# Two gated linear-attention blocks on one core: block B's reciprocals through DRAM, its scalings by row halves

## The chip, the cores and the metric

The kernel runs on one core of a Trainium2 chip. The metric is the device time of the whole program in microseconds; lower is better. The kernel before took 183.14 us, the median of three runs (183.08 to 183.65).

## The reference

Input x is [1, 2048, 640] in bf16. Two blocks A and B have weights of the same shapes, 32 heads of 20 columns each; both read A's x.

```python
def _A_ref(x, wqkv, wo):            # _B_ref is the same with B's weights
    q, k, v = ...                   # x @ wqkv, split in 3 x 32 heads x 20
    phi = lambda t: jnp.where(t > 0, t + 1, jnp.exp(t)) + 1e-6
    pq, pk = phi(q), phi(k)
    kv = jnp.einsum("bhsd,bhse->bhde", pk, v)
    z = jnp.einsum("bhsd->bhd", pk)
    num = jnp.einsum("bhqd,bhde->bhqe", pq, kv)
    den = jnp.einsum("bhqd,bhd->bhq", pq, z)[..., None] + 1e-6
    o = num / den
    return ... @ wo                 # o with its heads side by side
x = A_x
g = _sigmoid((x * gate_w).sum(-1, keepdims=True))
return g * _A_ref(x, A_wqkv, A_wo) + (1 - g) * _B_ref(x, B_wqkv, B_wo)
```

## The kernel before

The 2048 rows and 640 columns are cut in blocks of 128 (16 by 5). All tiles but a few DRAM ones stay on chip. `pk` holds phi(k) by rows; `pqT[0]` and `pqT[1]` hold phi(q) of A and B transposed, as [128, 5, 2048]. The order of the work on each engine is the order in which the program emits it: the scheduler is off (`manual_schedule`), and the framework adds the waits.

**The stages.** A's k and q come first, then the rest of A's q by a Strassen product (`q_strassen`). `g_strassen` computes G = x^T pk, from which KV is made with `wv`; in its midst, `z_rows` and `z_pass` sum pk into z, and `rec_pass` computes the denominators with `by_group` and takes their reciprocals through logarithms, with the gate (`ge`) added. Then the same for B. KV times `wo` gives one 640 x 640 matrix M for each block (`m_a`, `m_b`), six row blocks g each, stored to DRAM (`m_store` to `m_rows`) and loaded back in another row order (`m_load`). At the end, `Pair` computes pqT[0] M_A + pqT[1] M_B for eight pairs of row blocks, again by Strassen products p1 to p7.

**The reciprocals.** `rec_pass` leaves `rT`, [128, 512]: partition 32 j + h has head h's reciprocals of rows 512 j to 512 j + 511. For the scaling they must stand as `R`, [128, 4, 512]: partition 4 h + t has head h's, for t of 0 to 3 and all four j. A and B do this in two ways. For A, `norm_load` stores rT to the DRAM tile `r_rows` four times over (512 KB) and loads R from it with one DMA. For B, `norm_spread` multiplies rT with the 0/1 matrix `spread` in four matmuls (tiles exB) and ScalarE copies the result into R. `scale(b, m, part)` then multiplies the columns m of pqT[b] by R on VectorE, over all 2048 rows or a part of them.

**The order of the work around the change.** In `g_strassen(1, ...)`, B's turn, SyncE issues the load of M_A and then three loads of B's `wo` (`load_wo`) just ahead of `rec_pass`. VectorE computes `p_diff` (differences of pqT[0]'s two row halves into D3, a quarter `part[n]` of the first half at a time), scales A's last columns, adds partial products into the second half matrix `GT[1]` (L527 and L587), and scales B's columns: m of 0 and 1 by row halves, 2 and 3 in full, 4 later. `rest` is `kv_low`: the first three KV blocks with their masks, and `tm_first` (the difference of M_A's column halves into TM[0]) for three of five blocks. After `g_strassen`, `m_b` makes M_B's row blocks: two matmuls, then two copies of half a row each, on ScalarE or VectorE. The three upper KV blocks (tile ox, L624, `kv_mm`) stand between `m_b(2)` and `m_b(3)`. They read GT[1], whose last piece is L587's second addition. Then follow `tm_first` for the other blocks, the scaling of m = 4, `p_sums` (sums of pqT[0] and pqT[1] by quarters, k of 1, 2 and 4), the pairs' p1 and p5, the last `p_diff`, and `m_sum` (TM[2], TM[1], TM[3] from the loaded M_B). The pairs' p2, p7 and p6 read M_B, TM[2] and TM[1] in this order.

All the plain loads and stores named here go through SyncE's one queue.

Of the kernel before, what the change touches and what calls it, by code (L numbers as in the profile page):

```python
# [21 lines left out]
HB = 512  # L22
HF = D // 2
TW = 4
NG = 6
K6 = 120
EPS = 1e-6
# [6 lines left out]
def kernel(  # L34
# [52 lines left out]
    def ps(name, slot=None):  # L87

        return banks(ps_raw(name, slot))
# [11 lines left out]
    zE = persist.tile([P, 2 * D], BF16, name="zE")  # L101
    E4 = zE[:, D:2 * D]
    maskE = persist.tile([P, HF], BF16, name="maskE")
    spread = persist.tile([P, P], BF16, name="spread")
    R = persist.tile([P, 4, HB], BF16, name="R")
    kv6 = [persist.tile([P, D], BF16, name="kvA6")[:], zE[:]]
    lift = persist.tile([P, 1], FP32, name="lift")
# [26 lines left out]
    scratch = ctx.enter_context(tc.tile_pool(name="scratch", bufs=1, space=bass.MemoryType.DRAM))  # L134
    m_rows = scratch.tile([D, D], BF16, name="m_rows")
    g_rows = scratch.tile([2 * ST, P], FP32, name="g_rows")
    r_rows = scratch.tile([4, P, HB], BF16, name="r_rows")

    wq_dram = [A_wqkv.rearrange("(c p) f -> p c f", p=P), B_wqkv.rearrange("(c p) f -> p c f", p=P)]
    wo_dram = [A_wo, B_wo]  # L140
# [37 lines left out]
    for r in range(4):  # L178
        rows = slice(32 * r, 32 * r + 32)
        nc.gpsimd.tensor_copy(out=I4[rows], in_=ident[rows, rows])  # L180
    nc.gpsimd.tensor_copy(
        out=spread[:].rearrange("p (h t) -> p h t", t=TW), in_=I4[:, :, None].to_broadcast([P, H, TW])
    )
    nc.gpsimd.memset(maskE[:], 1.0)
    for lo in range(0, HF, K6):
        part = maskE[:, lo:min(lo + K6, HF)]
# [63 lines left out]
    class Phi:  # L250
# [10 lines left out]
                    self.lift(lifted_to, part)  # L261

        def lift(self, to, part):
            nc.scalar.activation(out=to, in_=part, func=ACT.Identity, bias=lift[:])

        def clamp(self):
            nc.vector.tensor_scalar(self.e, self.e, 1.0, EPS, op0=ALU.min, op1=ALU.add)  # L267
# [247 lines left out]
    def g_strassen(b, main, second, spare, rest=None):  # L515

        x11, x12 = [xn[:, k:k + hc, 0:ic] for k in (0, hc)]
        x22 = xn[:, hc:ST, ic:2 * ic]
        b11 = pk[:, 0:hc, 0:HF]
        b21, b22 = [pk[:, hc:ST, n * HF:(n + 1) * HF] for n in range(2)]  # L520
        lo, hi = GT

        def temp(name):
            return work.tile([P, 2, HF], FP32, tag="osb", name=name, bufs=3)

        def add(dst, pt, sb):
            nc.vector.tensor_tensor(out=dst, in0=pt[:, :, 0:HF], in1=sb[:], op=ALU.add)  # L527

        even, odd = ps("gs0", main), ps("gs1", second)
        sel = []  # L530
        g_prod(even, x11, b11, True)
        nc.scalar.copy(out=odd[:, :, 0:HF], in_=even[:, :, 0:HF])
        if b == 0:
            rest()
            zr = z_rows(0, spare)
            sq_sum(1, 0)
            g_prod(even, x12, b21, False)
            nc.scalar.copy(out=lo[:, 0:2, :], in_=even[:, :, 0:HF])
            sq_sum(2, 0)
            x_sum(3)  # L540
        else:
            m_a(5, 2)
            nc.sync.dma_start(out=M[0][:], in_=m_rows[:].rearrange("(p m) d -> p m d", m=DT))
            load_wo(1, nc.sync)
            scale(0, 3)
            zr = z_rows(1, spare)
        g_prod(odd, SX[2], TK[b][2], False, lambda: sel.append(z_pass(b, zr)))
        u2 = temp("u2")
        nc.scalar.copy(out=u2[:], in_=odd[:, :, 0:HF])
        if b == 1:  # L550
            scale(0, 4)
            p_diff(part[0])
            rts = rec_pass(b, sel[0], 2)
            k_sum(1, 1)
            for rows in part[1:3]:
                p_diff(rows)
            g_prod(even, x12, b21, False)
            nc.scalar.copy(out=lo[:, 0:2, :], in_=even[:, :, 0:HF])
            norm_spread(b, rts, (2, spare))
        else:  # L560
            k_sum(0, 1)
            norm_load(rec_pass(b, sel[0], 2))
            x_sum(4)
            for k in (3, 4):
                sq_sum(k, 0)
            tq_sums(1, (0, 1))
        g_prod(odd, SX[3], TK[b][3], False)
        u3 = temp("u3")
        nc.scalar.copy(out=u3[:], in_=odd[:, :, 0:HF])
        if b == 1:  # L570
            for rows, ms in ((slice(0, SH), (0, 1)), (slice(SH, S), (0, 1))):
                for m in ms:
                    scale(b, m, rows)
        even = ps("gs0", main)
        g_prod(even, SX[1], TK[b][1], True)
        add(hi[:, 2:4, :], even, u3)
        if b == 0:
            tq_sums(1, (2, 3))
        else:
            scale(b, 2)  # L580
            scale(b, 3)
        g_prod(odd, x22, TK[b][4], False)
        nc.scalar.copy(out=lo[:, 2:4, :], in_=odd[:, :, 0:HF])
        for ns in ((0, 1),) if b == 0 else ((0,), (1,)):
            g_prod(even, SX[4], b22, False, None, ns)
            for n in ns:
                nc.vector.tensor_tensor(out=hi[:, n, :], in0=even[:, n, 0:HF], in1=u2[:, n], op=ALU.add)  # L587
            if b == 1 and ns == (0,):
                rest()

    def z_rows(b, slot=None):

# [36 lines left out]
    def kv_mask(b, banks, g0, g1):  # L629

        n, hf = rows_in(g0), g0 // 3
        at = slice(blocks[g0].start, blocks[g1 - 1].stop)
        part = slice(at.start - hf * HF, at.stop - hf * HF)
        nc.vector.tensor_tensor(out=kv6[b][:n, at], in0=banks[hf][:n, part], in1=maskE[:n, part], op=ALU.mult)
# [24 lines left out]
    def m_b(g, banks):  # L659

        to = m_block(1, g, banks, held["mb"][:, g, :] if g < DT else None)
        n = to.shape[0]
        for hf, copy in enumerate((nc.scalar.copy, nc.scalar.copy if g in (1, 2, 5) else nc.vector.tensor_copy)):
            copy(out=to[:, hf * HF:(hf + 1) * HF], in_=banks[hf][:n, 0:HF])
        m_store(g, to)

# [10 lines left out]
    def rec_pass(b, zsel, slot):  # L677

        pt = ps(f"den{'AB'[b]}", slot)
        by_group(pt[:, 0, :], zsel, pqT[b])  # L680
        rT = work.tile([P, HB], BF16, tag="rT", name="rT", bufs=1)
        ds = [(slice(n * RB, (n + 1) * RB), work.tile([P, RB], FP32, tag="d1", name="d1")) for n in range(2)]
        for part, d1 in ds:
            nc.scalar.activation(out=d1[:], in_=pt[:, 0, part], func=ACT.Ln, scale=LOGS, bias=tiny[:])
        for part, d1 in ds:
            nc.vector.scalar_tensor_tensor(
                out=d1[:], in0=d1[:], scalar=-2.0 * math.log(LOGS), in1=ge[:, b, part], op0=ALU.add, op1=ALU.add
            )
            nc.scalar.activation(out=rT[:, part], in_=d1[:], func=ACT.Exp, scale=-1.0)
        return rT  # L690
# [4 lines left out]
    def p_diff(rows):  # L695

        up = slice(SH + rows.start, SH + rows.stop)
        add_rows(D3[:, :, rows], pqT[0][:, :, rows], pqT[0][:, :, up], ALU.subtract)
# [12 lines left out]
    def tm_first(cs):  # L711
        add_rows(TM[0][:, cs], M[0][:, cs, HF:D], M[0][:, cs, 0:HF], ALU.subtract)
# [9 lines left out]
        else:  # L722
            add_rows(TM[3][:], b[:, :, lo], TM[1][:], ALU.subtract)

    def norm_load(rT):

        nc.sync.dma_start(
            out=r_rows[:].rearrange("j (h t) n -> (j h) t n", t=TW), in_=rT[:, None, :].to_broadcast([P, TW, HB])
        )
        nc.sync.dma_start(out=R[:], in_=r_rows[:].rearrange("j p n -> p j n"))  # L730

    def norm_spread(b, rT, slots):

        pts = [ps(f"ex{'AB'[b]}", s) for s in slots]
        for j in range(4):
            rows = slice(32 * j, 32 * j + 32)
            nc.tensor.matmul(
                pts[j // 2][:, j % 2, :], lhsT=spread[rows, :], rhs=rT[rows, :], start=True, stop=True,
            )
        for jj in range(2):  # L740
            nc.scalar.copy(out=R[:, 2 * jj:2 * jj + 2, :], in_=pts[jj][:])

    def scale(b, m, part=slice(0, S)):

        rec = R[:].rearrange("p j n -> p (j n)")
        nc.vector.tensor_tensor(out=pqT[b][:, m, part], in0=pqT[b][:, m, part], in1=rec[:, part], op=ALU.mult)
# [195 lines left out]
    with tc.manual_schedule():  # L942
# [113 lines left out]
        def kv_low():  # L1056
            kv = cells(ps("kvB", 2))
            kv_mm(1, kv, range(3))
            kv_mask(1, kv, 0, 2)
            kv_mask(1, kv, 2, 3)  # L1060
            tm_first(slice(0, 3))

        g_strassen(1, 1, 0, 3, kv_low)
        new_stage(None)
# [11 lines left out]
            kv_mm(1, [None, acc["x"][g > 3]], [g], (2, 3, 4, 0, 1))  # L1076
        for g in range(3, 6):
            kv_mask(1, [None, acc["x"][g > 3]], g, g + 1)
        pairs[4].p1(acc["w"][0], (0, 1))
        m_b(3, [acc["w"][1], acc["x"][0]])  # L1080
        pairs[4].p1(acc["w"][0], (2,))
# [3 lines left out]
        pairs[4].p1_out()  # L1085
        m_load(0, 3, nc.sync)
        m_load(3, 6, nc.sync)
        tm_first(slice(3, DT))
        scale(1, 4)
        for rows, ks in ((0, (1,)), (1, (1,)), (2, (1,)), (0, (2, 4))):  # L1090
            p_sums(part[rows], ks)
        for k, to in ((5, None), (6, acc["x"][0]), (7, acc["w"][1]), (2, acc["z"][0]), (3, acc["z"][1])):
            pairs[k].p1(to)
        held["p5"] = wpool.tile([P, 4, HF], FP32, tag="wv", name="p5s")
        pairs[0].p1()
        pairs[2].p5(spare[0])
        pairs[3].p5(acc["w"][1])
        pairs[1].p1()
        pairs[4].p5(spare[0])
        pairs[5].p5(acc["z"][1])  # L1100
        for p in pairs[0:2]:
# [3 lines left out]
        acc["y"] = [bank(inner, f"oy{n}") for n in range(2)]  # L1105
        TM[3] = wpool.tile([P, DT, HF], BF16, tag="wk", name="TM3")
        p_sums(part[1], (2, 4))
        p_diff(part[3])
        for k in (2, 1, 3):
            m_sum(k)  # L1110
        for p in pairs[0:2]:
# [60 lines left out]
```

## Time and profile before

| | before |
|---|---|
| median of three runs | 183.14 us (183.08, 183.14, 183.65) |
| profiled execution: span, first to last instruction | 181.6 us; its own time is not listed apart from that |
| TensorE busy | 177.7 us, 98% |
| VectorE busy | 148.3 us, 82% |
| ScalarE busy | 107.9 us, 59% |
| GpSimd busy | 5.0 us, 3% |
| DMA | 18.85 MB, 104 GB/s on the mean |
| granted TensorE clock | 1.000 |

The profile is of one execution, in microseconds from the first instruction. PE is TensorE, PEld its weight loads, DVE VectorE, ACT ScalarE, POOL GpSimd and SP SyncE. A row of the timeline is: start, length, engine, line of the kernel, operation, out<-in with the tiles' names, shapes, count, and in brackets the idle time before it with what ended it. Several like instructions in a row are one row; then the length runs from the first's start to the last's end. A row of the chain of waits is: start, length, what. A row of DMA issues on the page is: out<-in, queue, count, KB each, and the median us from the issue to the landing. A row of the table by windows is: the window, PE busy, then busy time and count of PE, PEld, DVE, ACT, POOL, then the granted clock, the busy share of the DMA engines and GB/s. Tiles that share memory can show under an older name: SQ is also D3, xT is also the sums' place, and T is a sum of pk.

### The profile page before, as it was taken

The numbers are of one execution on the slowest core, as the hardware profiler recorded it, in microseconds if no ns is written. First come the engines' busy times: TensorE is split into PE (matmuls) and PEld (weight loads), VectorE is DVE, ScalarE is ACT, GpSimd is POOL, SyncE is SP. The second block draws the span as 40 slices with busy tenths as digits, with TensorE's granted clock in tenths as the row PEclk, the third lists the DMA queues.
The fourth block names the chain that finished last, engine by engine and source line by source line (L and its number), as shares of the span: only waits on it lengthen the run. The fifth ranks groups of instructions, "written<-read, shape, count | busy, mean of one in ns | idle before, by whom it ended". The sixth has DMA issues, their size and how long they took to land.

```text
span 181.6 us, 3380 instructions
## 1 busy us (share of the span) xinstructions
PE 177.7 (98%) x1284; PEld 118.5 (65%) x1284; DVE 148.3 (82%) x268; ACT 107.9 (59%) x209; POOL 5.0 (3%) x21
## 2 busy tenths in 40 slices
PE   8999999999999999999999999999999999999993
PEld 3666656655666677676666655765678777777772
DVE  0478988999999896799898987997988988686764
ACT  2066579976884512785868696964814755466210
POOL 8300000000000000000000000000000000000000
PEclk9999999999999999999999999999999999999999
DMA  5995448985102733005000000043901660322132
GB/s 172 298 178 88 93 112 251 370 173 141 48 0 58 244 120 115 0 0 180 5 0 0 0 4 0 13 146 84 291 12 31 176 159 0 110 88 96 72 131 90
DMA packets 21602, 18.85 MB, mean 104 GB/s; under 512 B 9298, under 2 KB 21074, under 8 KB 21586
## 3 DMA queue, kind: packets, MB, share of 16 engines
q1 hardware_dynamic: 20722, 17.82, 35.7%
q10 hardware_dynamic: 864, 0.82, 1.3%
q8 instruction: 10, 0.16, 0.4%
q14 instruction: 6, 0.05, 0.1%
HBM read 11.86 MB, written 4.80 MB: 92 GB/s over the span
## 4 chain that ended last, share of the span: by engine, by line
PE 93%; DMA 4%; DVE 1%; issue 0%
PE gs L510 17%; PE kB L290 12%; PE q L408 11%; PE kA L290 11%; PE qA L343 7%; PE oy L757 6%; PE oz L757 5%; PE ox L757 4%; PE ow L757 4%; PE q L343 3%; DMA wkA<-in_A_wqkv_dram 2%; PE gB L480 2%; PE gA L480 2%; DMA xn<-in_A_x_dram 2%; PE qB L343 1%; PE mA L640 1%
## 5 line engine op out<-in xcount | busy, mean ns | idle before, releaser
L290 PEld LDWEIGHTS <-xT 128*128 128x128 bf16 x320 | 30.9, 97 | 15.4 <-issue 0.4
L267 DVE TENSOR_SCALAR e<-e 128x640 bf16<-128x640 bf16 (+2 forms) x58 | 19.6, 339 | 6.1 <-ACT e L259 5.5
L290 PE MATMUL kB<-wkB,xT 128*128 128x320 bf16 x160 | 24.2, 299 | 0.0
L290 PE MATMUL kA<-wkA,xT 128*128 128x320 bf16 (+1 forms) x160 | 23.4, 299 | 0.2 <-DMA wkA<-in_A_wqkv_dram 0.2
L259 ACT ACTIVATE e<-q 128x512 bf16<-128x512 f32 x26 | 15.7, 603 | 5.2 <-PE q L408 4.1
L510 PEld LDWEIGHTS <-xn 128*128 128x128 bf16 x128 | 12.2, 98 | 6.0 <-issue 1.3
L259 ACT ACTIVATE e<-kA 128x640 bf16<-128x640 f32 x16 | 11.3, 713 | 7.8 <-PE kA L290 7.7
L259 ACT ACTIVATE e<-kB 128x640 bf16<-128x640 f32 x16 | 11.4, 710 | 7.5 <-PE kB L290 7.3
L343 PE MATMUL qA<-xT,wqA 128*128 128x512 bf16 x60 | 13.4, 379 | 0.0
L343 PEld LDWEIGHTS <-wqA 128*128 128x128 bf16 x64 | 7.5, 117 | 5.9
L278 DVE SCALAR_TENSOR_TENSOR pk<-kB,e 128x640 bf16<-128x640 f32 x12 | 9.9, 823 | 1.0
L820 ACT COPY u<-ox 128x320 f32<-128x320 f32 x8 | 3.4, 425 | 11.4 <-PE ox L757 11.4
L757 PEld LDWEIGHTS <-xT 128*128 128x128 bf16 x85 | 8.1, 98 | 2.9
L757 PEld LDWEIGHTS <-pqTA 128*128 128x128 bf16 x85 | 8.0, 98 | 2.8
L762 DVE TENSOR_TENSOR osb<-oz,u 128x320 bf16<-128x320 f32 (+2 forms) x18 | 8.0, 453 | 2.2 <-PE oz L757 1.8
L757 PEld LDWEIGHTS <-pqTB 128*128 128x128 bf16 x80 | 7.8, 98 | 3.0
L510 PE MATMUL gs<-pk,xn 128*128 128x320 bf16 x64 | 9.4, 299 | 0.0
L278 DVE SCALAR_TENSOR_TENSOR pk<-kA,e 128x640 bf16<-128x640 f32 x10 | 8.2, 823 | 0.9
L426 DVE TENSOR_TENSOR q<-q,p 128x512 f32<-128x512 f32 x12 | 8.3, 692 | 0.8 <-PE q L408 0.6
L259 ACT ACTIVATE e<-qA 128x1024 bf16<-128x1024 f32 x6 | 6.2, 1027 | 4.2 <-PE qA L343 3.9
L480 PEld LDWEIGHTS <-xn 128*128 128x128 bf16 x64 | 6.3, 98 | 3.0
L510 PEld LDWEIGHTS <-S 128*128 128x128 bf16 x64 | 6.0, 98 | 2.5 <-issue 0.3
(183 smaller groups left out, 348.1 us busy)
## 6 DMA issues: line engine op xcount, KB each, us to landing
out_dram<-osb SPq DMA_DIRECT2D x14, 160.0 KB, 1.8
xn<-in_A_x_dram SPq DMA_DIRECT2D x3, 640.0 KB, 6.7
wvA<-in_A_wqkv_dram SPq DMA_DIRECT2D x1, 800.0 KB, 12.0
wkB<-in_B_wqkv_dram SPq DMA_DIRECT2D x1, 800.0 KB, 4.5
wqB<-in_B_wqkv_dram SPq DMA_DIRECT2D x1, 800.0 KB, 5.3
wvB<-in_B_wqkv_dram SPq DMA_DIRECT2D x1, 800.0 KB
MA<-m_rows SPq DMA_DIRECT2D x1, 800.0 KB, 5.3
MB<-m_rows SPq DMA_DIRECT2D x2, 400.0 KB, 4.3
```

What stands on the lines that cost most here:

```text
L259: nc.scalar.activation(out=to, in_=part, func=ACT.Exp)
L267: nc.vector.tensor_scalar(self.e, self.e, 1.0, EPS, op0=ALU.min, op1=ALU.add)
L278: nc.vector.scalar_tensor_tensor(out=dst, in0=src, scalar=1.0 + EPS, in1=e, op0=ALU.add, op1=ALU.max)
L290: nc.tensor.matmul(pt[:, hf, 0:n], lhsT=xT[:, c, i * P:(i + 1) * P], rhs=wk[b][:, c, hf * HF:hf * HF + n], start=(c == 0), stop=(c == DT - 1),
L343: nc.tensor.matmul(dst, lhsT=mixed(wq[b][:, c, :], m), rhs=xT[:, c, n * HB:(n + 1) * HB], start=first, stop=last,)
L408: nc.tensor.matmul(dst, lhsT=left(c), rhs=right(c), start=first and k == 0, stop=k == len(cs) - 1, skip_group_check=not first,)
L426: nc.vector.tensor_tensor(out=dst, in0=src, in1=sb, op=ALU.add)
L480: nc.tensor.matmul(pt[:, hf, 0:HF], lhsT=xn[:, i, c * P:(c + 1) * P], rhs=pk[:, i, hf * HF:(hf + 1) * HF], start=(i == 0), stop=(i == ST - 1),
L510: nc.tensor.matmul(pt[:, n, 0:HF], lhsT=left[:, i, n * P:(n + 1) * P], rhs=right[:, i, :], start=(first and i == 0), stop=(i == hc - 1), s ...
L757: nc.tensor.matmul(dst, lhsT=left[:, c, r0:r0 + P], rhs=right[:, c, :], start=(first and c == 0), stop=(c == DT - 1), skip_group_check=not ...
L762: nc.vector.tensor_tensor(out=dst, in0=acc, in1=sb, op=ALU.add)
L820: nc.scalar.copy(out=self.u2[:], in_=self.at("x"))
```

## The change

- B's reciprocals go through DRAM as A's do. `norm_spread`, the matrix `spread` and ScalarE's two copies are gone. The new `norm_store` stores rT once (128 KB), each block to its own DRAM tile; the new `norm_load` loads R with four DMAs of 128 KB, one for each j, whose source repeats each row four times. A uses the same two functions.
- B's scalings are all by row halves (10 instead of 4 halves and 3 full ones) and later: m of 0 and 1, first half, where m of 2 and 3 were; m = 2, first half, in the middle of the last two additions to GT[1]; m of 3 and 4, first half, and 0, second half, behind the KV masks; the other second halves behind `m_load`.
- `tm_first` moves ahead, in one piece, to where the scalings of m of 0 and 1 were, and so does the last `p_diff`.
- `m_b` copies both halves on ScalarE for all g but 0, where g of 3 and 4 had one half on VectorE.
- The first `p_sums` come in the order of quarters 1, 2, 0 instead of 0, 1, 2; p1 of pairs 0 and 1 come together ahead of the first p5, and p5 of pair 3 goes to another PSUM bank.
- The bias of the lifts (`Phi.lift`, L264) is a number instead of a tile.

```diff
-    spread = persist.tile([P, P], BF16, name="spread")
-    r_rows = scratch.tile([4, P, HB], BF16, name="r_rows")
+    r_rows = [scratch.tile([4, H, HB], BF16, name=f"r_rows{b}") for b in "AB"]
...
-            nc.scalar.activation(out=to, in_=part, func=ACT.Identity, bias=lift[:])
+            nc.scalar.activation(out=to, in_=part, func=ACT.Identity, bias=1.0 + EPS)
...
         if b == 1:
             scale(0, 4)
             p_diff(part[0])
-            rts = rec_pass(b, sel[0], 2)
+            norm_store(1, rec_pass(b, sel[0], 2))
+            norm_load(1, range(4))
             k_sum(1, 1)
             for rows in part[1:3]:
                 p_diff(rows)
             g_prod(even, x12, b21, False)
             nc.scalar.copy(out=lo[:, 0:2, :], in_=even[:, :, 0:HF])
-            norm_spread(b, rts, (2, spare))
         else:
             k_sum(0, 1)
-            norm_load(rec_pass(b, sel[0], 2))
+            norm_store(0, rec_pass(b, sel[0], 2))
+            norm_load(0, range(4))
...
         if b == 1:
-            for rows, ms in ((slice(0, SH), (0, 1)), (slice(SH, S), (0, 1))):
-                for m in ms:
-                    scale(b, m, rows)
+            tm_first(slice(0, DT))
+            p_diff(part[3])
...
-            scale(b, 2)
-            scale(b, 3)
+            for m in (0, 1):
+                scale(b, m, slice(0, SH))
...
             if b == 1 and ns == (0,):
                 rest()
+                scale(b, 2, slice(0, SH))
...
-        for hf, copy in enumerate((nc.scalar.copy, nc.scalar.copy if g in (1, 2, 5) else nc.vector.tensor_copy)):
+        for hf, copy in enumerate((nc.scalar.copy, nc.scalar.copy if g else nc.vector.tensor_copy)):
...
-    def norm_load(rT):
-        nc.sync.dma_start(
-            out=r_rows[:].rearrange("j (h t) n -> (j h) t n", t=TW), in_=rT[:, None, :].to_broadcast([P, TW, HB])
-        )
-        nc.sync.dma_start(out=R[:], in_=r_rows[:].rearrange("j p n -> p j n"))
+    def norm_store(b, rT):
+        nc.sync.dma_start(out=r_rows[b][:].rearrange("j h n -> (j h) n"), in_=rT[:])
+    def norm_load(b, js):
+        for j in js:
+            nc.sync.dma_start(
+                out=R[:, j, :], in_=r_rows[b][j][:, None, :].to_broadcast([H, TW, HB])
+            )
...
             kv_mask(1, kv, 2, 3)
-            tm_first(slice(0, 3))
...
             kv_mask(1, [None, acc["x"][g > 3]], g, g + 1)
+        for m, rows in ((3, slice(0, SH)), (4, slice(0, SH)), (0, slice(SH, S))):
+            scale(1, m, rows)
...
-        tm_first(slice(3, DT))
-        scale(1, 4)
-        for rows, ks in ((0, (1,)), (1, (1,)), (2, (1,)), (0, (2, 4))):
+        for m in range(1, DT):
+            scale(1, m, slice(SH, S))
+        for rows, ks in ((1, (1,)), (2, (1,)), (0, (1,)), (0, (2, 4))):
...
-        pairs[0].p1()
+        for p in pairs[0:2]:
+            p.p1()
         pairs[2].p5(spare[0])
-        pairs[3].p5(acc["w"][1])
-        pairs[1].p1()
+        pairs[3].p5(acc["z"][0])
...
         p_sums(part[1], (2, 4))
-        p_diff(part[3])
```

More of the change, by code (lines that the diff above doesn't have):

```diff
@@ L180 @@
         nc.gpsimd.tensor_copy(out=I4[rows], in_=ident[rows, rows])
-    nc.gpsimd.tensor_copy(
-        out=spread[:].rearrange("p (h t) -> p h t", t=TW), in_=I4[:, :, None].to_broadcast([P, H, TW])
-    )
     nc.gpsimd.memset(maskE[:], 1.0)
@@ L723, in m_sum @@
             add_rows(TM[3][:], b[:, :, lo], TM[1][:], ALU.subtract)
-    def norm_load(rT):
-        nc.sync.dma_start(
-            out=r_rows[:].rearrange("j (h t) n -> (j h) t n", t=TW), in_=rT[:, None, :].to_broadcast([P, TW, HB])
[L729 to L738, printed above, removed]
-            )
-        for jj in range(2):
-            nc.scalar.copy(out=R[:, 2 * jj:2 * jj + 2, :], in_=pts[jj][:])
+    def norm_store(b, rT):
[4 more added lines that the diff above has]
+                out=R[:, j, :], in_=r_rows[b][j][:, None, :].to_broadcast([H, TW, HB])
+            )
     def scale(b, m, part=slice(0, S)):
```

## Prediction, made before the result was known

> **What bounds the kernel now.** I read three views in this order: the page's first, second and fourth part, to see which engine sets the end; the chain of waits in order of time around the change, to see whether that engine ever stops; and the timeline of the other engines there, to see how much room each has.
>
> ```profile
> span 181.6 us, 3380 instructions
> PE 177.7 (98%) x1284; PEld 118.5 (65%) x1284; DVE 148.3 (82%) x268; ACT 107.9 (59%) x209; POOL 5.0 (3%) x21
> PE 93%; DMA 4%; DVE 1%; issue 0%
> ```
>
> TensorE is busy for 98% and carries 93% of the chain; the rest of the chain is the first loads and the last additions. VectorE has 82%, so it has room on average, but an average says nothing about one place. The chain around the change (start, length, what):
>
> ```profile
> 128.49 0.33 PE exB L737 x4
> 128.82 7.71 PE gs L510 x56
> ...
> 138.91 0.27 PE mB L640 x2
> 139.18 0.74 PE ox L624 x15
> ```
>
> Each piece begins where the one before ended (128.49 and 0.33 is 128.82, 138.91 and 0.27 is 139.18), in the rows left out too. TensorE does not stop here, so this stretch gets shorter only by matmuls taken out, and longer by every input that comes late. Now VectorE, ScalarE and SyncE beside it (start, length, instruction, in brackets the idle time before it):
>
> ```profile
> 127.23 0.78 ACT L689 ACTIVATE rT<-d 128x256 bf16<-128x256 f32 x2
> 127.56 0.42 SPq L873 DMA_DIRECT2D woB<-in_B_wo_dram  x1
> 128.88 1.56 DVE L693 TENSOR_TENSOR SQ<-pqTA 128x1280 bf16<-128x1280 bf16 x2
> 130.35 2.49 DVE L746 TENSOR_TENSOR pqTB<-pqTB,R 128x1024 bf16<-128x1024 bf16 x4
> 133.38 0.82 DVE L527 TENSOR_TENSOR GT<-gs,u 128x640 bf16<-128x640 f32 x1 [0.54 <-PE gs L510]
> 134.12 2.35 DVE L746 TENSOR_TENSOR pqTB<-pqTB,R 128x2048 bf16<-128x2048 bf16 x2
> 136.57 0.49 DVE L587 TENSOR_TENSOR GT<-gs,u 128x320 bf16<-128x320 f32 x1
> 137.30 0.55 DVE L634 TENSOR_TENSOR zE<-kvB,maskE 120x240 bf16<-120x240 f32 x2 [0.24 <-PE kvB L624]
> 137.78 0.65 DVE L693 TENSOR_TENSOR TM<-MA 128x960 bf16<-128x960 bf16 x1
> 138.40 0.49 DVE L587 TENSOR_TENSOR GT<-gs,u 128x320 bf16<-128x320 f32 x1
> 139.02 0.90 PE L624 MATMUL ox<-GT,wvB 128*120 128x120 bf16 x15
> ```
>
> The place to watch is the last two rows. The second half of GT is added on VectorE until 138.40 + 0.49 = 138.89; the matmuls that read it (ox, the upper KV blocks) start at 139.02, at once. There is no slack between them. Whatever makes that addition later makes TensorE stop.
>
> **The change, part by part.**
>
> *Removed from TensorE:* the four exB matmuls that spread rT over partitions, 0.33 us in the chain. Everything behind them moves up by 0.33 us if its inputs do. The POOL copy that makes the spread matrix was off the chain from the start.
>
> *Removed from ScalarE:* the two copies of exB into R. ScalarE was not late here. The biases of the lifts become a number; whatever ScalarE gains by that is hidden, since the chain gives ScalarE no share at all. Two half-row copies of M_B (g of 3 and 4) move from VectorE to ScalarE.
>
> ```profile
> 141.23 0.74 ACT L664 CAST m<-mB 80x320 bf16<-80x320 f32 x2
> 142.68 0.34 SPq L649 DMA_DIRECT2D m_rows<-m  x1
> ```
>
> ScalarE has eleven copies instead of nine. In a row they take 0.74 / 2 = 0.37 us each, so the last ends at 141.97 + 2 x 0.37 - 0.33 = 142.4 where it was 141.97; its store leaves at 142.68 today. I count zero; without that cover it is 0.4 us on the load of M_B.
>
> *A's half:* the store shrinks from 512 to 128 KB, and the load becomes four loads of 128 KB. The first user is the scaling at 71.44.
>
> ```profile
> 66.89 0.38 SPq L730 DMA_DIRECT2D R<-r_rows  x1
> 71.44 1.22 DVE L746 TENSOR_TENSOR pqTA<-pqTA,R 128x2048 bf16<-128x2048 bf16 x1
> 55.80 2.83 SPq L238 DMA_DIRECT2D ge<-g_rows  x4
> r_rows<-rT SPq DMA_DIRECT2D x1, 512.0 KB, 3.3
> R<-r_rows SPq DMA_DIRECT2D x1, 512.0 KB, 3.8
> m_rows<-MA SPq DMA_DIRECT2D x4, 150.0 KB, 2.0
> ge<-g_rows SPq DMA_DIRECT2D x4, 128.0 KB, 2.9
> ```
>
> Today's load leaves at 66.89, when the store of 3.3 us has landed, so the store left at 63.6. A store of 128 KB is nearest to the 150 KB ones: 2.0 us, landing at 65.6. Four issues took 2.83 us for ge, so the last leaves by 68.0 and lands by 68.0 + 2.9 = 70.9, before 71.44. Zero.
>
> *B's half, the costly part.* Today R is filled on chip and VectorE starts scaling at 130.35. Now R takes a round trip through DRAM. The store cannot leave before rT, 127.23 + 0.78 = 128.01, and SyncE is free of woB at 127.56 + 0.42 = 127.98; so it leaves at 128.0. But it stands behind woB and the load of M_A in the same queue:
>
> ```profile
> 131.00:132.00 1.00, 1.00 (x9) 0.72 (x8) 1.00 (x3) 0.74 (x2) 0.00 (x0) 1.00 0.87 164
> 132.00:133.00 1.00, 1.00 (x10) 0.71 (x8) 0.84 (x2) 0.00 (x0) 0.00 (x0) 1.00 0.11 22
> woB<-in_B_wo_dram SPq DMA_DIRECT2D x2, 300.0 KB, 5.5
> wvA<-in_A_wqkv_dram SPq DMA_DIRECT2D x1, 800.0 KB, 12.0
> woA<-in_A_wo_dram SPq DMA_DIRECT2D x1, 200.0 KB, 10.7
> 28.14 0.98 SPq L863 DMA_DIRECT2D wvA<-in_A_wqkv_dram  x1
> 31.78 0.80 SPq L873 DMA_DIRECT2D woA<-in_A_wo_dram  x1
> ```
>
> The last two columns of the first rows are the busy share of the DMA engines and GB/s: they work until a little after 132. And the queue is served in order: wvA left at 28.14 and landed at 40.1; the small woA part left at 31.78 and landed at 42.5, not ahead of it. So the store lands with woB's end: bounds are 130.0 (128.0 + 2.0, no queue) and 134.6 (132.6 + 2.0, all of its latency after the queue). I take 133.4: woB's second part left before 127.56 and took 5.5 us, so up to 133.0, and the window from 132 to 133 has little of it, so 132.6; the store's 128 KB behind it take 0.8 us at the 164 GB/s of that time. Then the loads: the first leaves at 133.4, the second, which completes the first row half, 0.4 us later, landing 2.0 (the 150 KB rows) to 2.9 us (ge) after: I take 2.5, between them, since a lone load of 512 KB took 3.8. That is 133.4 + 0.4 + 2.5 = 136.3, and with a tenth for the semaphore R's first half is usable at T = 136.4.
>
> What VectorE does meanwhile: tm_first (0.65 + 0.48 in two pieces today) and the last p_diff (0.78, half of the 1.56) fill 130.35 to about 132.1; then the 0.82 addition at 133.05 (up by 0.33). From 133.9 its next instruction is the scaling of row half 0, and VectorE waits for T with the first GT addition, the masks, a third scaling and the second GT addition queued behind. From T on: two half scalings at 2.49 / 4 = 0.62, 1.24; the GT addition 0.45; the masks 0.48 (137.30 to 137.78); one half scaling in the place of tm_first, 0.62 (137.78 to 138.40); the second addition 0.49. It ends at T + 3.28 = 139.7 instead of 138.89. TensorE's ox follows it without slack, so TensorE is **0.8 us later than today**, the 0.33 us it had won included. Break-even is at T + 3.28 = 138.89, T = 135.6; up to T = 135.3 the addition waits for TensorE alone and the whole 0.33 us is kept.
>
> *The later scalings:* seven row halves come after the masks, where today are one full scaling, the two M_B copies and 0.48 of tm_first.
>
> ```profile
> 149.79 0.99 DVE L693 TENSOR_TENSOR TM<-MB,MA 128x1600 bf16<-128x1600 bf16 x1 [0.60 <-DMA MB<-m_rows]
> 150.70 2.07 DVE L693 TENSOR_TENSOR TM<-MB,TM 128x1600 bf16<-128x1600 bf16 x2
> 152.12 0.84 PE L757 MATMUL ox<-TM,xT 128*128 128x320 bf16 x5
> 139.96 0.43 DVE L634 TENSOR_TENSOR zE<-ox,maskE 120x120 bf16<-120x120 f32 x2 [0.18 <-PE ox L624]
> 142.97 2.29 DVE L693 TENSOR_TENSOR pqTA<-pqTA,pqTB 128x1280 bf16<-128x1280 bf16 x3
> ```
>
> Today the p_sums begin at 142.97, and VectorE waits 0.60 us for M_B before 149.79. With the masks ended at 139.96 + 0.43 = 140.4 and 7 x 0.62, they begin at 144.7, 1.8 us later; a p_diff (0.78) is gone from before the m_sums, and the wait (0.60) swallows another part: the m_sums come 1.8 - 0.78 - 0.60 = 0.4 us later. TM1 was done at 150.70 + 2.07 / 2 = 151.7, against 152.12 of its reader: 0.4 us of slack. If TensorE itself is 0.8 us later, VectorE's chain moves with it and M_B's does too (its first copy stands behind the second GT addition): no second bill. If R is in time, TensorE comes 0.33 us earlier than today, and up to 0.4 us may be due here.
>
> *Sum:* 181.6 + 0.8 = 182.4 for the profiled execution. The median of the three runs is 183.14, 1.5 us outside the span; so 183.14 + 0.76 = **183.9 us**.
>
> **The rivals.** *(1) R is in time (T up to 135.3): 183.14 - 0.33 = 182.8 us, not slower.* For it: by the lower bounds, a store that does not queue and a load of 2.0 us, T is 130.0 + 0.4 + 2.0 + 0.1 = 132.5. Against it: the in-order rows above. It decides at T = 135.6. The Trainium skill, "DMA: Bandwidth & Descriptors", Latency and other measured facts, gives 0.6 us to the first byte of a DMA from this queue; an estimate from that page, with 0.3 us for 128 KB, would have the second load land at 134.7 and this rival win. The trace's own loads of 128 KB took 2.9 us, which speaks against it. Chance 0.32.
> *(2) R is later still:* the scalings wait for all four loads, 0.8 us more, or each transfer meets its upper bound, T = 137.2 to 137.9: 184.7 to 185.4 us. Against the first: today the first half scaling started at 130.35, before the second half of R was copied. Chance 0.14.
> *(3) VectorE's late chain binds* though R is in time: the 0.4 us of the late scalings, or the 0.4 us of M_B's copies, meets a TensorE that has no slack left after moving up 0.33 us: 182.8 + 0.4 = 183.2 us. Chance 0.05.
>
> **How the numbers follow.** Forecast (T between 135.9 and 137.0, 183.4 to 184.5): 0.45; rival 1 0.32, rival 2 0.14, rival 3 0.05, and 0.04 for what I don't see. A measurement here tells about 0.3%, 0.55 us. Faster by that would need more than the 0.33 us of matmuls taken out, and no other matmul goes: only the unseen 0.04. Within it lie rivals 1 and 3 and the forecast below T = 136.2 (0.08): 0.45. Slower: the rest of the forecast, 0.37, and rival 2: 0.51. The likeliest is 183.9; the range runs from 182.6, rival 1 with some room for the spread of the runs, to the middle of rival 2, 185.0; the forecast's own is 183.4 to 184.5.
>
> **What would show it.** Right: a VectorE row at the first half scaling of pqTB with idle time before it put down to DMA R<-r_rows, of about 2.5 us, ending near 136.4; then a gap of TensorE before m_b or ox at 138 to 140, of 1.1 us, that the chain of waits gives to VectorE or DMA; no exB rows. Wrong in size: R's loads that land before 135.3 and a chain that is all TensorE. Wrong in place: TensorE stopping first at the readers of TM1 or of M_B near 150, or A's first scaling waiting near 71.

## The result, and the profile after

The changed kernel takes 185.01 us, the median of six runs (184.23 to 187.56), beside 183.11 us of the kernel before on the same chip (183.01 to 183.65). The ratio is 1.009, with an interval of 1.0063 to 1.0117; it leaves out the longest run, in which the clock was lower, as the ratios below leave out every run over 1.5% above the fastest of its kernel. So the change costs 1.2 to 2.1 us. The prediction was 183.9, in 182.6 to 185.0; the median lies at the upper end of that.

From the page of the changed kernel: the span, the busy time of each engine, the slices of TensorE and of its granted clock, the shares of the chain of waits, and the group of B's scalings (busy time and mean ns of one, then the idle time just before and what ended it).

```profile
span 184.7 us, 3382 instructions
PE 179.0 (97%) x1280; PEld 119.3 (65%) x1280; DVE 147.4 (80%) x268; ACT 104.4 (57%) x209; POOL 4.8 (3%) x20
PE   8999999999999999999999999999959999999993
PEclk9999999999999999999999999999996999999999
PE 89%; DMA 6%; DVE 1%; SPq 1%; issue 0%; DVEq 0%
L736 DVE TENSOR_TENSOR pqTB<-pqTB,R 128x1024 bf16<-128x1024 bf16 x10 | 6.3, 682 | 3.3 <-DMA R<-r_rowsB 3.3
```

Four matmuls fewer (1280 for 1284), yet the span is 3.1 us longer. Two slices tell why: in slice 30 TensorE falls to a half, and in slice 31 it is busy again, but its clock is not full. TensorE's share of the chain fell from 93% to 89%; DMA and the issue queues have taken most of it. One thing waits for DMA in the middle of the kernel, the scalings of B, and only once: 3.3 us in one piece. The view of TensorE's waits has the other end (who <- for whom: us, times, longest):

```profile
PE gs L506 <- DVE GT L583: 2.0, 1, 2.0
PE warm L202 <- PEq L1146: 0.8, 1, 0.8
```

TensorE stops once after its warm-up, for 2.0 us, at the last product of `g_strassen` (tile gs), for the first GT addition. The timeline shows what lies between (start, length, instruction, in brackets the idle time before it):

```profile
127.40 0.42 SPq L863 DMA_DIRECT2D woB<-in_B_wo_dram  x1
127.86 0.44 SPq L724 DMA_DIRECT2D r_rowsB<-rT  x1
132.69 0.82 DVE L523 TENSOR_TENSOR GT<-gs,u 128x640 bf16<-128x640 f32 x1 [0.88 <-PE gs L506]
133.72 2.47 SPq L729 DMA_DIRECT2D R<-r_rowsB  x4
136.81 1.29 DVE L736 TENSOR_TENSOR pqTB<-pqTB,R 128x1024 bf16<-128x1024 bf16 x2 [3.29 <-DMA R<-r_rowsB]
138.02 0.49 DVE L583 TENSOR_TENSOR GT<-gs,u 128x320 bf16<-128x320 f32 x1
138.56 2.27 PE L506 MATMUL gs<-pk,MB 128*128 128x320 bf16 x8 [1.98 <-DVE GT L583]
140.86 0.49 DVE L583 TENSOR_TENSOR GT<-gs,u 128x320 bf16<-128x320 f32 x1 [1.30 <-PE gs L506]
```

The store leaves at 127.86 right behind wo, its landing lets the loads go at 133.72, and VectorE stands before the first scaling until 136.81. Behind two scalings comes the first GT addition, and only when it is done does TensorE begin the second half of the product, which writes the tile that this addition reads. (By the code the addition reads the half n = 0 of the tile and these matmuls write the half n = 1; whether a tile for each half would spare the wait was not tried.) The eight matmuls then take 2.27 us, where the first half took 1.25. The table by windows (last three columns: granted clock, busy share of the DMA engines, GB/s) says why:

```profile
138.00:139.00 1.00, 0.44 (x2) 0.24 (x2) 1.00 (x5) 0.00 (x0) 0.00 (x0) 0.81 0.00 0
139.00:140.00 1.00, 1.00 (x5) 0.58 (x4) 0.56 (x1) 0.00 (x0) 0.00 (x0) 0.50 0.00 0
140.00:141.00 1.00, 1.00 (x6) 0.70 (x4) 0.14 (x1) 0.00 (x0) 0.00 (x0) 0.50 0.00 0
141.00:142.00 1.00, 1.00 (x6) 0.74 (x5) 0.85 (x2) 0.76 (x3) 0.00 (x0) 0.50 0.00 0
142.00:143.00 1.00, 1.00 (x18) 0.97 (x17) 0.28 (x1) 1.00 (x4) 0.00 (x0) 0.98 0.21 51
```

Behind the gap the clock is halved: 0.19 + 3 x 0.50 + 0.02 = 1.71 us lost, that is 3.4 us at half clock. To compare programs without their first loads and last stores, I take the time from the start of the first qA matmuls to the start of the last additions and call it the body; the chain of waits has both, of before and of after:

```profile
11.65 4.32 PE qA L343 x20
...
178.15 0.98 DVE osb L762 x3
```

```profile
11.51 4.32 PE qA L339 x20
...
181.26 0.98 DVE osb L752 x3
```

That is 166.50 us before and 169.75 after, 3.25 us more. The terms: -0.33 for exB, +1.98 for the gap, +1.71 for the clock make 3.36. Not every run pays for the clock: of the six, the profiled one (186.43) and the longest have a mean granted clock of 0.991 and 0.990, the other four 0.998 to 1.0 and 184.23 to 185.04 us. A mean of 0.991 over 184.7 us is 1.7 us, one such halved stretch.

### The profile page after: what moved, and what is told of

The parts are those of the page before. It is cut to its first block, busy times and chain, and to the rows that moved or that the text cites. A ratio compares the mean times of both kernels' runs of the same rounds, so it can differ in the third digit from the quotient of the medians.

```text
span 184.7 us, 3382 instructions
## 1 busy us (share of the span) xinstructions
PE 179.0 (97%) x1280; PEld 119.3 (65%) x1280; DVE 147.4 (80%) x268; ACT 104.4 (57%) x209; POOL 4.8 (3%) x20
## 4 chain that ended last, share of the span: by engine, by line
PE 89%; DMA 6%; DVE 1%; SPq 1%; issue 0%; DVEq 0%
PE gs L506 12%; PE kA L286 12%; PE kB L286 12%; PE q L404 11%; PE qA L339 7%; PE oy L747 6%; PE oz L747 6%; PE ox L747 4%; PE ow L747 4%; DMA r_rowsB<-rT 3%; PE q L339 3%; PE gB L476 2%; PE gA L476 2%; DMA xn<-in_A_x_dram 2%; DMA R<-r_rowsB 1%; PE qB L339 1%
## 5 line engine op out<-in xcount | busy, mean ns | idle before, releaser
L736 DVE TENSOR_TENSOR pqTB<-pqTB,R 128x1024 bf16<-128x1024 bf16 x10 | 6.3, 682 | 3.3 <-DMA R<-r_rowsB 3.3
```

## The experiments

Each kernel is timed against the kernel before on the same chip. Line numbers differ by a few between kernels.

**wo behind the round trip.** The changed kernel, but wo's three loads are issued behind the loads of R.

```diff
             nc.sync.dma_start(out=M[0][:], in_=...)
-            load_wo(1, nc.sync)
             scale(0, 3)
...
             norm_load(1, range(4))
+            load_wo(1, nc.sync)
             k_sum(1, 1)
```

> The changed kernel with one edit: the three loads of B's wo are issued behind B's store and loads of R instead of ahead of them. Theory Q (R is late because the store stands behind wo in SyncE's queue): the store leaves near 127.9 as before but lands near 130.2 instead of 133.7, R's first half near 133 instead of 136.8; VectorE's first half scaling starts at 133.6, right behind the 0.82 us addition, TensorE has no gap, and the time is 0.33 us under the kernel before: 182.8 us. Theory L (the late order of the scalings and M_B's copies on ScalarE cost the time): the time stays at 184.3 or more. If wo itself comes late (it is wanted at 137.9), m_b's first matmul waits, and the time lies between, with the gap at m_b.

182.94 us (182.57 to 184.10), before 183.44: ratio 0.9978, interval 0.9959 to 0.9997. Its timeline:

```profile
128.34 0.34 SPq L724 DMA_DIRECT2D r_rowsB<-rT  x1
130.11 1.18 SPq L729 DMA_DIRECT2D R<-r_rowsB  x2
133.99 1.28 DVE L736 TENSOR_TENSOR pqTB<-pqTB,R 128x1024 bf16<-128x1024 bf16 x2
136.44 0.49 DVE L583 TENSOR_TENSOR GT<-gs,u 128x320 bf16<-128x320 f32 x1 [1.16 <-PE gs L506]
```

The same store now takes 1.7 us (128.34 to before 130.11), not 5.8. The first scaling has no bracket: it waits for nothing. The first GT addition waits for TensorE, not the other way round, and TensorE has no gap there. So the whole loss hangs on what stands in front of the store. A repeat on another chip gave 183.04 us (182.38 to 183.85) beside 183.51, ratio 0.9986, 0.997 to 1.0002. By the two ratios that is 0.4 and 0.3 us below before, near the 0.33 us of exB. Of all kernels here this is the fastest; 2 us below the changed one, and below the one before by so little that one of the two intervals still touches 1.

> The kernel with wo behind once more, beside the one with A's old path: 182.6 to 183.2 us, and 0.3 to 0.5 us below the kernel before on this chip (the exB matmuls taken out are 0.33 us).

**The spread on chip again.** The changed kernel with `norm_spread` for B put back; the later scalings, the moved `tm_first` and `p_diff`, ScalarE's copies and A's half stay.

```diff
-            norm_store(1, rec_pass(b, sel[0], 2))
-            norm_load(1, range(4))
+            rts = rec_pass(b, sel[0], 2)
...
+            norm_spread(b, rts, (2, spare))
```

> The changed kernel with B's reciprocals spread on chip again (four matmuls, two copies on ScalarE), all else of the change kept. Theory Q: R is there by 131, no wait on VectorE, no gap on TensorE, the 0.33 us of matmuls are back: 183.1 us, as the kernel before, within 0.3 us. Theory L: the late scalings, tm_first and p_diff ahead, and ScalarE's copies carry the loss: 184.3 us or more, with TensorE waiting for TM1 or M_B near 150.

183.59 us (183.08 to 183.88) beside 183.44, ratio 1.0009, 0.9994 to 1.0023, and in its trace TensorE does not stop between its start and its end. All of the reordering costs nothing that can be told from none. The loss is B's trip through DRAM.

**The DRAM path alone.** The kernel before with `norm_store` and `norm_load` for both blocks, and none of the later scalings.

```diff
-            rts = rec_pass(b, sel[0], 2)
+            norm_store(1, rec_pass(b, sel[0], 2))
+            norm_load(1, range(4))
...
-            norm_spread(b, rts, (2, spare))
```

> The kernel before with the round trip through DRAM alone (A's and B's R by one store and four loads); B's scalings stay where they were, at 130.4. Theory Q: R's first half is usable at 136.8, its last quarter near 138.3; VectorE waits from 130.4 for it, four half scalings, 2.5 us, then the addition to GT that frees the PSUM tile of the next product, which TensorE wants at 135.0, ends near 141: a gap of TensorE of about 5 us, and with the clock at half for 3.4 us behind it another 1.7: 188 to 190 us. Theory L: without the late order the DRAM path costs little: 182.8 to 184 us.

190.37 us (190.09 to 190.63), ratio 1.0377, 1.0347 to 1.0406, a little more than the 188 to 190 that I expected. From its timeline, and then from its windows:

```profile
137.04 2.52 DVE L751 TENSOR_TENSOR pqTB<-pqTB,R 128x1024 bf16<-128x1024 bf16 x4 [6.76 <-DMA R<-r_rowsB]
140.35 2.29 PE L510 MATMUL gs<-pk,MB 128*128 128x320 bf16 x8 [5.49 <-DVE GT L527]
```

```profile
138.00:139.00 1.00, 0.00 (x0) 0.00 (x0) 1.00 (x3) 0.00 (x0) 0.00 (x0) 0.60 0.00 0
...
144.00:145.00 1.00, 1.00 (x5) 0.60 (x4) 0.99 (x3) 0.00 (x0) 0.00 (x0) 0.50 0.00 0
145.00:146.00 1.00, 1.00 (x9) 0.83 (x7) 0.45 (x2) 0.18 (x1) 0.00 (x0) 0.98 0.00 0
```

R comes at 137.0, as in the changed kernel, but here an earlier addition (L527, 640 columns) stands behind the scalings, and TensorE stops for 5.5 us, until 140.35; the clock is at half from 138.2, while TensorE still stands, until 145. The later scalings are what keeps the loss at 1.9 us instead of 7: they are not a cost of the change but its cover.

**The gap filled.** The changed kernel with 14 matmuls of no use behind kvB, into a PSUM tile that is free there, so that TensorE is not idle before gs.

```diff
             kv_mm(1, kv, range(3))
+            for i in range(14):
+                nc.tensor.matmul(kv[1][:, 0:HF], lhsT=xn[:, i, 0:P], rhs=pk[:, i, 0:HF], ...)
```

> The changed kernel with 14 more matmuls of 320 columns (1.9 us, their output is not used) in the place where TensorE stood still, behind the lower KV blocks. The wait for R stays. Theory C (part of the loss, and its spread from 184.2 to 187.6 us, is the granted clock that falls to half after the gap): every run has a clock of 1.0 and a span of 182.9, 1.3 us over the kernel before, 184.4 us, with the spread of the kernel before. Against it: if the gap itself is all, median and spread stay as the changed kernel's, 185.0.

185.05 us (184.41 to 185.35), ratio 1.0089, 1.0066 to 1.0111. TensorE's wait before gs is short now:

```profile
PE gs L506 <- DVE GT L583: 0.5, 1, 0.5
```

No run has a lower clock, and none is above 185.35. So the halved clock belongs to the long runs of the changed kernel. Its runs at full clock, 184.23 to 185.04 us, pay for the wait itself: the filler takes the place of the gap and ends no sooner.

**The changed kernel once more**, to see how often the clock falls.

> The changed kernel once more, to see its spread beside the others: with R late, its time should lie at 184 to 187 us, each run by when R lands, and by whether the granted clock falls behind the gap of 2 us.

186.43 us (184.65 to 187.43), ratio 1.0141, 1.0094 to 1.0188. Three of six runs have a clock of 1.0 (184.65, 184.70, 185.72), three of 0.991 (187.14 to 187.43). The profiled one has a full clock, with this wait:

```profile
PE gs L506 <- DVE GT L583: 1.8, 1, 1.8
```

The first profiled one, with 1.98, was halved. With the first six that is five halved runs of twelve; none of twelve with the gap filled (above) or split in two (next). The five have a median of 187.27 us, the other seven of 184.70. That is 2.6 us apart, more than the 1.7 of the clock. The rest may be longer stops in the halved runs: one of 2.5 us stands in the halved profile of the store on another queue, below. Four of these five have no trace, so this stays open.

**The additions last.** The changed kernel, but the first GT addition is emitted behind the second half of the product, together with the second addition, so that TensorE needs not wait for the tile.

```diff
+            if b == 1 and ns == (0,):
+                rest()
+                scale(b, 2, slice(0, SH))
+                continue
-            for n in ns:
+            for n in range(2):
                 nc.vector.tensor_tensor(out=hi[:, n, :], in0=even[:, n, 0:HF], ...)
-            if b == 1 and ns == (0,):
-                rest()
-                scale(b, 2, slice(0, SH))
```

> The changed kernel with VectorE's addition to the first half of the last GT product emitted behind TensorE's second half of that product, next to the other addition. R stays late. In the changed kernel TensorE stopped at that second half, because it writes the PSUM tile which the addition reads, and the addition stood behind the scalings that wait for R. Theory P (the PSUM tile is what TensorE waits for first): no gap there; TensorE then stops at the M_B blocks for the masks (near 138.6) and at the upper KV blocks for GT (VectorE: 136.8 + 1.24 + 0.48 + 0.62 + 0.9 = 140.0), so the gap moves and the end is about as late: 184.3 us, 1.2 over the kernel before, in two shorter gaps, and the granted clock stays at 1.0. Rival: the gap stays at the second half of the product, and so does the time, 185.0.

184.56 us (184.26 to 185.10) beside 183.28, ratio 1.007, 1.0055 to 1.0084. TensorE's waits:

```profile
PE ow L638 <- DVE zE L632: 1.0, 1, 1.0
PE warm L202 <- PEq L1147: 0.8, 1, 0.8
PE ox L622 <- DVE GT L587: 0.5, 1, 0.5
```

Now the stop stands where the prediction had put it, at the masks and the ox matmuls, in two pieces. The body is 167.87 us, 1.37 more than before, and every run has a clock of 0.998 or more. So it is the first GT addition that TensorE stopped for in the changed kernel. Most of the loss stays, since R is late all the same: the median is 0.1 us under that of the changed kernel's seven runs at full clock.

**The store on another queue.** The changed kernel with B's store issued by ScalarE.

```diff
-        nc.sync.dma_start(out=r_rows[b][:]...
+        eng = nc.scalar if b == 1 else nc.sync
+        eng.dma_start(out=r_rows[b][:]...
```

> The changed kernel with B's store of the reciprocals issued by ScalarE, on its own queue; wo stays ahead on SyncE's queue, and R's four loads stay behind it there. Theory Q1 (the store is late because it stands behind wo in the same queue): it lands near 130.5 instead of 133.7, R's loads go out from 130.6 and land behind wo's end, the second near 134.5, and the time is between 182.8 and 183.4. Theory Q2 (the DMA engines are busy with M_A and wo until 132, whatever the queue): the store lands near 133.5 again and the time stays at 185.0.

185.05 us (184.44 to 187.82), ratio 1.008, 1.0063 to 1.0098: no gain. Its four runs at full clock, 184.44 to 185.28 us, lie where those of the changed kernel do. The timeline of its profiled execution, one of two with a halved clock, and TensorE's wait in it:

```profile
128.35 0.33 ACTq L725 DMA_DIRECT2D r_rowsB<-rT  x1
132.96 0.99 DVE L690 TENSOR_TENSOR TM<-MA 128x1600 bf16<-128x1600 bf16 x1 [2.22 <-DMA MA<-m_rows]
135.06 2.48 SPq L730 DMA_DIRECT2D R<-r_rowsB  x4
```

```profile
PE gs L506 <- DVE GT L583: 2.5, 1, 2.5
```

From a queue with nothing ahead of it the store still took 6.6 us to land, and R's loads left at 135.06, where theory Q2 has the store land near 133.5. The load of M_A was later too, and VectorE waited for it. So in this execution the store stands behind the bytes on the DMA engines, not behind SyncE's list. The Trainium skill, "DMA: Bandwidth & Descriptors", Issuing engines are not separate DMA queues, says this: DMAs from the scalar, sync or gpsimd engine run on the same 16 DMA engines. The trace agrees: 6.6 us from ScalarE's queue, 5.8 from SyncE's.

**A part of wo behind.** The changed kernel with only the last 200 KB of wo behind R's loads (`load_wo` has an argument for which parts it loads: first the two of 300 KB, then the last).

```diff
-            load_wo(1, nc.sync)
+            load_wo(1, nc.sync, False)
...
             norm_load(1, range(4))
+            load_wo(1, nc.sync, True)
```

> The changed kernel, with the last 200 KB of wo (one of its three loads) issued behind R's loads; 600 KB stay ahead of the store. If the store waits for the bytes ahead of it, it lands 200 KB / 164 GB/s = 1.2 us before the 133.72 of the changed kernel, near 132.5, and R is usable at T = 135.5 to 135.6. The break-even that the prediction worked out, at the second GT addition, is T = 135.6: no gap of TensorE or one below 0.1 us, 182.9 to 183.1 us. The theory of the first GT addition, behind which the second product half waits for its PSUM tile: there TensorE stops from T = 136.58 - 1.70 = 134.9 on, so a gap of 0.6 to 0.7 us before the second half of gs (L506), put down to DVE GT L583, no half clock behind so short a gap, and 183.3 to 183.7 us.

183.97 us (183.63 to 187.45) beside 183.51, ratio 1.0026, 1.0014 to 1.0039.

```profile
127.72 0.35 SPq L725 DMA_DIRECT2D r_rowsB<-rT  x1
132.82 2.48 SPq L730 DMA_DIRECT2D R<-r_rowsB  x4
136.08 1.29 DVE L737 TENSOR_TENSOR pqTB<-pqTB,R 128x1024 bf16<-128x1024 bf16 x2 [2.63 <-DMA R<-r_rowsB]
137.82 1.25 PE L506 MATMUL gs<-pk,MB 128*128 128x320 bf16 x8 [1.31 <-DVE GT L584]
```

R came at 136.08, later than the 135.5 that I expected: 200 KB less in front spared the store 0.75 us, not 1.2 (5.04 us instead of 5.79). The place decides between the theories all the same. The stop is at gs, 1.31 us, and there is none at ox. TensorE was free at 137.82 - 1.31 = 136.51 and had to wait until 1.74 us behind the first scaling's start, so the stop begins at T = 134.8; the changed kernel gives the same, 138.56 - 1.98 - 1.75 = 134.8. Both programs reach this place earlier than the kernel before: their 16 gs matmuls behind denB start at 125.82 and 125.89, there at 126.14. On the clock of the kernel before, the stop begins at 135.1. The prediction has it begin at 135.3; its 135.6 is the break-even, with the 0.33 us of exB in it. The body is 167.42 us (11.44 to 178.86), 0.92 more than before; by gap and exB it would be 1.31 - 0.33 = 0.98. One run of the ten, not the profiled one, has a clock of 0.989 and 187.45 us.

**A's half alone.** The kernel before, with `norm_store` and `norm_load` for A only; then once more, beside the kernel with wo behind and A's old path.

```diff
-            norm_load(rec_pass(b, sel[0], 2))
+            norm_store(0, rec_pass(b, sel[0], 2))
+            norm_load(0, range(4))
```

> The kernel before with A's part of the change alone: rT stored once, 128 KB, and R loaded by four DMAs. As predicted: the last quarter lands near 69.5, before 71.4, nobody waits, 0 us, the time of the kernel before within 0.3 us. Rival: SyncE's longer issues put wq or the next loads late, and VectorE's scaling waits near 71: 183.5 us or more against 183.1.

> The kernel before with A's half alone, once more. If A's half costs 0.5 us: 0.3 to 0.7 us above the kernel before again. If the 0.5 us came with the program's first loads and its last store, which differ from run to run: within 0.3 us of the kernel before.

> The changed kernel with wo's loads behind R's loads for B, and for A the path of the kernel before (one store of 512 KB, one load). If A's half by itself costs 0.5 us, as its kernel alone measured: 0.4 to 0.6 us below the repeat of the kernel with wo behind and A's new path, which runs beside it. If A's half costs nothing, as its trace from 12 us to 178 us says: the two within 0.2 us of each other.

A's half alone: 183.80 us (183.53 to 184.76) beside 183.28, ratio 1.0034, 1.0018 to 1.005; repeated, 183.76 beside 183.51, ratio 1.0022, 1.0009 to 1.0035. I had expected nothing. But with wo behind the round trip, A's old path is no faster: 183.47 (182.70 to 183.93; ratio 0.9994, 0.998 to 1.0008) beside 183.04 of the same kernel with the new path (0.997 to 1.0002). By the medians it is the slower one, but the intervals overlap. So one edit has a cost in one program and none in another; the chain's ends tell where it lies. Of A's half alone, first kernel and repeat:

```profile
11.86 4.32 PE qA L343 x20
...
178.35 0.98 DVE osb L767 x3
```

```profile
11.86 4.32 PE qA L343 x20
...
178.50 0.98 DVE osb L767 x3
```

The bodies are 166.49 and 166.64 us, before 166.50; the scaling of A, at 71.65, waits for nothing. What is longer is the start (11.86 for 11.65) and the end: from 179.33 to the span's 182.1 us are 2.8 us, where before it was 2.5. A's half issues nothing in either. The other pair has bodies of 166.50 (old path) and 166.51, and spans of 182.2 and 181.7 us. So between these programs up to 0.5 us is in the first loads and the last stores; why a program has the longer ones stays open.

The body of the kernel with wo behind was 165.95 us in its first profile and 166.51 in the repeat, and this has its own reason, a stop at the third matmul pair of `m_b(0)` (tile mB), seen in the repeat and, here, in the timeline of the kernel with A's old path, with the DMA issues of its stretch from 132 to 142 us below (KB, us to the landing):

```profile
134.06 0.42 SPq L869 DMA_DIRECT2D woB<-in_B_wo_dram  x1
139.14 0.44 PE L636 MATMUL mB<-woB,zE 80*80 80x320 bf16 x2 [0.39 <-DVE MBr L660]
```

```profile
woB<-in_B_wo_dram SPq DMA_DIRECT2D x1, 200.0 KB, 5.0
```

The row names a copy on VectorE. In the first profile of the kernel with wo behind, though, the same matmuls ran at 138.61, before that copy began at 138.67, so they don't need it. What they read is wo's last part: issued at 134.06 with 5.0 us to its landing, it came at 139.0. The pair starts 0.83 us behind the pair before it in the repeat (138.04 and 138.87), 0.82 with A's old path (138.32 and 139.14) and 0.27 in the first profile (138.34 and 138.61): 0.56 us from the first profile to the repeat, all by which their bodies differ. Putting wo behind has moved the wait: what is late next is wo itself, by some 0.6 us in two of the three profiles. That reading rests on the order of two rows and a landing; a kernel with wo's last part sent first, or the load of M_A moved instead, wasn't tried.

## Why the prediction was right, and where not

**Right: the round trip is late, and by how much.** The store left at 127.86 (predicted 128.0); the loads could go at 133.7 (133.4); R was usable at T = 136.8 (136.4); VectorE waited 3.3 us (2.5, as it was free at 133.5 and not at 133.9). The two experiments with wo moved confirm that the bytes of wo ahead of the store make it late. The reason that the prediction gave is confirmed only in part: it read the in-order rows of wvA and woA as the order of one queue, and from ScalarE's queue the store was no sooner. The estimate from the Trainium skill, "DMA: Bandwidth & Descriptors", Latency and other measured facts, by which 0.6 us to a first byte would let rival 1 win, is not borne out: the loads of R took 2.2 to 2.6 us to land. Yet rival 1 is what the kernel with wo behind does: no wait, 182.94 us, for 182.8 predicted.

**Wrong: the place of the stop, and so its price.** The step that failed is "TensorE's ox follows it without slack, so TensorE is 0.8 us later than today", with the break-even at T = 135.6. I followed who reads GT and didn't ask which matmuls wait until the additions have read their tile. The second half of the product has to wait for the first addition, at T + 1.7, before the masks, a scaling and the second addition have a say. On the clock of the kernel before, TensorE stops from T = 135.1 on, where the prediction has 135.3. T itself was the larger error: 136.81 is 137.06 on that clock, 0.7 us later than 136.4. For that T the prediction's rule gives a stop of 1.8 us (137.06 - 135.3); it was 1.98. The kernel with the additions last is the other side of this: there the stop is at the masks and ox. At T of 137.3 on the same clock (137.57, with the gs matmuls behind denB at 126.42) its body is 1.37 us longer than before's; that of the changed kernel's second profile, with T of 136.9 (136.71; 125.98), is 1.39 us longer (11.60 to 179.49). So at the same T the earlier stop costs 0.2 to 0.4 us more.

**Missing: the clock.** No term of the sum had it. In the profiled run the stop is followed by 3.4 us at half clock, 1.7 us more; five of twelve runs have the mean clock of such a stretch, and they are the ones from 186.4 to 187.6. The Trainium skill, "TensorE: Matmul & The Clock Gate", Part 1, has the clock halved after an idle window of some 3.4 us and full again after a busy one as long, and its rule is no idle gaps over some 3.4 us. The length of the halved stretch agrees (3.4 us); the gap does not: one of 1.98 us was enough here, 1.8 in another run was not. The window that the Trainium skill has there is free-running, so that its phase differs from run to run, and that would fit a penalty that comes and goes; but so would stops of different length, and no run here shows the window itself.

**Right: what was counted at zero.** With R in time and wo behind, the kernel gained 0.4 and 0.3 us by its ratios, near exB's 0.33; with A's old path as well nothing is clear (0.9994). The late scalings: p_sums begin at 147.74 instead of 142.97 while ox is 3.1 us later, so 1.7 us by themselves (1.8 predicted), and the m_sums 0.4 (0.4); from the changed kernel's timeline:

```profile
147.74 2.30 DVE L690 TENSOR_TENSOR pqTA<-pqTA,pqTB 128x1280 bf16<-128x1280 bf16 x3
153.27 0.99 DVE L690 TENSOR_TENSOR TM<-MB,MA 128x1600 bf16<-128x1600 bf16 x1
```

No wait of TensorE follows from them, nor from ScalarE's copies (the kernel with the spread put back). A's loads were all issued by 67.7, and its scaling at 71.23 did not wait. Rival 3 did not come; rival 2's time did, but not by its mechanism: T was below its 137.2 (only just, with 137.06 on the clock of the kernel before), and the scalings did not wait for all four loads. That the median lies at the range's end is in part luck: this end stood there for rival 2.

**The numbers.** 185.01 is 1.1 us above the forecast: 0.7 from T, 0.2 to 0.4 from the place of the stop, and a rest from the runs with a halved clock and from a start and an end that differ by half a microsecond between runs; this rest I can't divide further.

## What to carry to other kernels

A value sent through DRAM comes when the bytes already on the DMA engines have gone, so before a round trip is put on a tight path, look at what was issued in the microseconds ahead of it, and move that behind; a second queue did not help here. When a wait is placed, follow both the readers of what it delays and the writers that must wait for its readers: the earlier of the two sets the price. And price a stop of TensorE of about 2 us with what may follow it, here another 1.7 us at half clock.

## What the runs showed of the hardware that I had not expected

- The clock fell to half behind a gap of 1.98 us, for 3.4 us, and not behind gaps of 1.8 and 1.3 us in other profiles. Of the kernel with 1.3 us one run of ten has the mean clock of a halved stretch (0.989); it has no trace, so its own gap isn't known. In a gap of 5.5 us the clock fell 3.3 us behind the gap's start and stayed at half twice as long (138.2 to 145.0).
- 128 KB stored behind some 1.6 MB issued in the 3.2 us ahead of it took 5.8 us, behind 200 KB less 5.0, with wo out of the way 1.7; a load of 128 KB whose source repeats each row took 2.2 to 2.6 us to land, and its issue 0.53 to 0.62 us, where one of woB's 200 KB took 0.42.
- The same store from ScalarE's queue was no sooner (6.6 us, one execution), and VectorE had M_A only 7.7 us after the issue of its load (125.23 to 132.96), where in the changed kernel it read it after 5.4 us without a wait (124.67 to 130.09).
